# Batch 0 loaded by head halves, its first FFN tiles in another order, and batch 1's last 64 positions behind batch 2's keys by values

## The chip, the cores and the metric

The kernel runs on one core of one Trainium2 chip. The metric is the device time of an execution in microseconds. Lower is better. In this document PE is TensorE, DVE is VectorE, ACT is ScalarE, POOL is GpSimd and SP is SyncE.

## What is computed

The reference is a linear attention over 8 batches of 576 positions with 8 heads of 64, followed by a gated FFN on all 4608 positions:

```python
r = np.maximum(x, 0.0)                       # for q and for k
phi = np.concatenate([r * c, r * s], -1)     # c, s: cos and sin of pi/2 * position / S
kv = np.einsum('bhsf,bhsd->bhfd', k_p, v)    # keys by values, 128 x 64 a head
z = np.sum(k_p, axis=2)
num = np.einsum('bhsf,bhfd->bhsd', q_p, kv)
den = np.einsum('bhsf,bhf->bhs', q_p, z)[..., None] + 1e-06
x = (num / den)                              # to (4608, 512)
out = (gelu(x @ w_gate) * (x @ w_val)) @ w_out      # 512 -> 1536 -> 512
```

Inputs and output are 32-bit floats; the matmuls run on bf16.

## The kernel before

The program is written out by hand in its order: what the source issues first on an engine runs first there, and engines meet only through semaphores.

A batch has 576 positions in tiles t = 0 to 4 of 128, 128, 128, 128 and 64. For each batch, `sk` (L351) and `sq` (L348) scale k and q by the cosine (which = 0) and sine (which = 1) on VectorE ("v") or ScalarE ("s"), `cast_v` (L139) turns v into bf16, and `kv_half` (L151) multiplies keys by values for heads 0 to 3 or 4 to 7, 20 matmuls of 65 columns (the 65th column is the sum z). `numer` (L193) does the eight numerator matmuls of a tile (`numer_mm`, L168) and its normalisation (`norm`, L177: den, reciprocal, and a multiplication that writes the tile `xb`). Then x has to be transposed into `xT`, either on TensorE with an evacuation (`x_by_pe`, L336) or by a DMA from SP (`turn_x`, L201; for the last tile of a batch GpSimd copies the result into place, L209). q is transposed by TensorE (`q_by_pe`, L320, and `q_evac`, L328) or by DMA (`turn_q`, L143).

The FFN runs in blocks n of 576 (n = 0) or 512 positions and 12 tiles jt of 128 hidden columns. `gate` (L214) is four matmuls and a Gelu on ScalarE, `value` (L225) four matmuls and a product on VectorE into `hT`. `o_tile` (L266) is the 12 output matmuls for 128 positions. An output tile can begin 64 positions ahead of its block, so `carry(n)` (L242) has GpSimd copy the last 64 columns of block n's `hT` to the front of the other `hT` buffer.

Each `gate`, `value`, `numer` and transpose names its PSUM bank by hand. A matmul into a bank waits until the bank's last reader is done.

**The start.** The source loads batch 0 in this order on SP (one piece of k on ScalarE's queue): k of heads 0 to 3, k of heads 4 to 7, q of tiles 0 and 1, v of heads 0 to 3, v of heads 4 to 7, the rest of q. Each is two transfers (odd and even partitions). The weights come on GpSimd's queue (`load_w`, L304), held back by a small copy on ScalarE (L360) that waits for q. TensorE runs matmuls on zeros (`dummies`, L125) until real work is there, and a few between. Then batch 0's attention and block 0's FFN are interleaved by hand (L355 to L443), so that gates on the first positions begin while later tiles of x are still computed. In L401 to L407, `X(t, bank, engine)` is `x_by_pe` of tile t, and `Y(t, bank)` is `numer` of tile t.

**Block 0's end.** Batch 1's k and v are loaded behind a part of `w_out` (L449). After block 0's last value, batch 1's keys are scaled, its v cast, and its keys by values put between output tiles (L478 to L492). Batch 1's tiles 0 to 3 are computed there too; its tile 4 is left for block 1:

```python
    mid[1][3].append(L(attn_step, 1, 5))
```

`mid[n][jt]` is what runs between gate and value of tile jt in block n, `after[n][jt]` what follows the value. In block 1, batch 2's keys are scaled and its v cast in `after[1][0]` to `after[1][3]`, and its keys by values are in `after[1][4]` (banks 6 and 7). From block 2 on every block holds the same work for the next batch.

Of the kernel before, what the change touches and what calls it, by code (L numbers as in the profile page):

```python
# [10 lines left out]
BF16 = mybir.dt.bfloat16  # L11
# [5 lines left out]
def kernel(  # L17
# [19 lines left out]
    NJ = 4  # L37
# [50 lines left out]
    pos_i = sb.tile([128, NJ + 1], mybir.dt.int32, name="pos_i")  # L88
    par_i = sb.tile([128, 1], mybir.dt.int32, name="par_i")
    load(kf, k, 0, 0, 4, nc.scalar)  # L90
    load(kf, k, 0, 4, 8)
    nc.vector.memset(junk, 0.0)
    nc.gpsimd.iota(par_i, pattern=[[1, 1]], base=0, channel_multiplier=1)
    nc.gpsimd.iota(pos_i, pattern=[[2, NJ + 1]], base=0, channel_multiplier=9)
    half_pi = sb.tile([128, 1], FP32, name="half_pi")
    nc.gpsimd.memset(half_pi, math.pi / 2.0)
    nc.gpsimd.memset(qf[:, :, NJ], 0.0)
    nc.gpsimd.memset(vf[:, :, NJ], 0.0)
    load(qf, q, 0, j1=2)
    load(vf, v, 0, 0, 4)  # L100
    load(vf, v, 0, 4, 8)
    load(qf, q, 0, j0=2)

# [35 lines left out]
    def cast_v(b, h0, h1, eng="v"):  # L139
        cp = nc.vector.tensor_copy if eng == "v" else nc.scalar.copy  # L140
        cp(vx[b % 2][:, :, h0:h1, 0:D], vf[:, h0:h1].rearrange("p h j d -> p j h d"))  # L141
# [9 lines left out]
    def kv_half(b, g, bank, eng="s"):  # L151
        for h in range(4 * g, 4 * g + 4):
            for j in range(NJ + 1):
                nc.tensor.matmul(  # L154
                    ps[:, bank, (h % 4) * (D + 1):(h % 4 + 1) * (D + 1)],
                    lhsT=kp[:, j, h, :],
                    rhs=vx[b % 2][:, j, h, 0:D + 1],
                    start=(j == 0), stop=(j == NJ),
                )
        if eng is not None:  # L160
            kv_evac(b, g, bank, eng)

    def kv_evac(b, g, bank, eng):
        src = ps[:, bank, 0:4 * (D + 1)].rearrange("p (h e) -> p h e", e=D + 1)
        dst = kv[b % 2][:, 4 * g:4 * g + 4, 0:D + 1]
        (nc.scalar.copy if eng == "s" else nc.vector.tensor_copy)(dst, src)

    def numer_mm(b, t, bank, g, rows=128):  # L168
        for h in range(4 * g, 4 * g + 4):
            nc.tensor.matmul(  # L170
                ps[0:rows, bank + g, (h % 4) * (D + 1):(h % 4 + 1) * (D + 1)],
                lhsT=qT[b % 2][:, t, h, 0:rows],
                rhs=kv[b % 2][:, h, 0:D + 1],
                start=True, stop=True,
            )

    def norm(xb, bank, g0, g1, rows=128):  # L177

        n = g1 - g0
        nd = ps[0:rows, bank + g0:bank + g1, 0:4 * (D + 1)].rearrange("p g (h e) -> p g h e", e=D + 1)  # L180
        den = rot.tile([128, 2, 4], FP32, name="den")
        nc.vector.tensor_scalar(den[0:rows, 0:n], nd[:, :, :, D], EPS, None, op0=ALU.add)  # L182
        rec = rot.tile([128, 2, 4], FP32, name="rec")
        nc.vector.reciprocal(rec[0:rows, 0:n], den[0:rows, 0:n])
        nc.vector.tensor_tensor(  # L185
            xb[0:rows, g0:g1], nd[:, :, :, 0:D],
            rec[0:rows, 0:n, :, None].to_broadcast([rows, n, 4, D]), op=ALU.mult,
        )

    def new_xb():  # L190
        return rot.tile([128, 2, 4, D], BF16, name="xb", bufs=4)
# [33 lines left out]
    def value(n, jt, c0, w, vb):  # L225

        p0 = starts[n] + c0
        for ct in range(CT):
            nc.tensor.matmul(  # L229
                ps[:, vb, 0:w], lhsT=wv_sb[:, ct, jt * 128:(jt + 1) * 128],  # L230
                rhs=xT[:, ct, p0:p0 + w], start=(ct == 0), stop=(ct == CT - 1),
            )
# [95 lines left out]
    def q_evac(b, j, bank, eng, h0=0, h1=H):  # L328
        qb = ps[:, bank, :].bitcast(BF16).rearrange("p (h t) -> p h t", h=H)
        cp = nc.vector.tensor_copy if eng == "v" else nc.scalar.copy  # L330
        if j < NJ:
            cp(qT[b % 2][:, j, h0:h1], qb[:, h0:h1])  # L332
        else:
            cp(qT[b % 2][:, j, h0:h1, 0:64], qb[:, h0:h1, 0:128:2])

    def x_by_pe(b, t, xb, bank, eng, c0=0, c1=CT):  # L336
        p0 = b * S + t * 128
        cp = nc.vector.tensor_copy if eng == "v" else nc.scalar.copy
        xb2 = xb.rearrange("p g h d -> p (g h d)")
        rows = 128 if t < NJ else 64  # L340
        view = ps[:, bank, 0:256].bitcast(BF16).rearrange("p (c t) -> p c t", c=CT)
        for ct in range(c0, c1):
            nc.tensor.transpose(  # L343
                out=view[:, ct, 0:rows], in_=xb2[0:rows, ct * 128:(ct + 1) * 128], identity=ident[0:rows, 0:rows],
            )
        cp(xT[:, c0:c1, p0:p0 + rows], view[:, c0:c1, 0:rows])

    def sq(j, which, eng, *h):  # L348
        scale(Q, j, which, eng, *h)

    def sk(j, which, eng, *h):  # L351
        scale(K, j, which, eng, *h)


    dummies(26)  # L355
    for h0 in (0, 4):
        for j in range(NJ + 1):
            sk(j, 0, "v", h0, h0 + 4)
            sk(j, 1, "v" if j < 2 else "s", h0, h0 + 4)
    nc.scalar.copy(wg_sb[0:2, 0, 0:1], qf[0:2, 7, 1, D - 1:D])  # L360
    load_w(0, 2)
    load_w(2, 4)
    load_w(4, 8)
    for j in range(2):
        sq(j, 0, "v"), sq(j, 1, "s")
        q_by_pe(0, j, j, None)
    dummies(3)
    q_evac(0, 0, 0, "v")
    cast_v(0, 0, 2, "v")
    cast_v(0, 2, 4, "s")  # L370
    kv_half(0, 0, 4, None)
    q_evac(0, 1, 1, "v")
    dummies(2)
    cast_v(0, 4, 6, "v")
    cast_v(0, 6, 8, "s")
    kv_evac(0, 0, 4, "v")
    kv_half(0, 1, 5, "s")
    x0, x1 = new_xb(), new_xb()
    numer_mm(0, 0, 6, 0)
    norm(x0, 6, 0, 1)  # L380
    dummies(1, 4)
    numer_mm(0, 0, 6, 1)
    sq(2, 1, "s")
    norm(x0, 6, 1, 2)
    sq(2, 0, "v")
    numer_mm(0, 1, 0, 0)
    numer_mm(0, 1, 0, 1)
    norm(x1, 0, 0, 2)
    x_by_pe(0, 0, x0, 4, "s", 0, 2)
    dummies(2, 5)  # L390
    x_by_pe(0, 0, x0, 4, "s", 2, 4)
    q_by_pe(0, 2, 3, None)

    nc.gpsimd.tensor_copy(tiny[0:1, 1:2], x0[0:1, 1, 3, D - 1:D])
    load_w(8, 12)
# [5 lines left out]
    def X(t, bank, eng):  # L401
        return lambda: x_by_pe(0, t, xs[t], bank, eng)

    def Y(t, bank):
        def f():
            xs[t] = numer(0, t, bank, 128 if t < NJ else 64)
        return f  # L407

    gate(0, 0, 0, 128, 5)
    gate(0, 1, 0, 128, 4)  # L410
    X(1, 2, "s")()
    q_evac(0, 2, 3, "v")
    sq(3, 0, "v"), sq(3, 1, "s")
    value(0, 0, 0, 128, 6)
    value(0, 1, 0, 128, 7)
    Y(2, 0)()
    gate(0, 0, 128, 128, 5)
    gate(0, 1, 128, 128, 4)
    value(0, 0, 128, 128, 2)
    value(0, 1, 128, 128, 3)  # L420
    q_by_pe(0, 3, 6, "s")
    gate(0, 2, *A, 5)
    X(2, 0, "v")()
    sq(4, 1, "s"), sq(4, 0, "v")
    gate(0, 3, *A, 4)
    value(0, 2, *A, 7)
    Y(3, 0)()
    value(0, 3, *A, 2)
    q_by_pe(0, 4, 3, "s")
    gv_unit(0, 0, 256, 128, 5, 6)  # L430
    gv_unit(0, 1, 256, 128, 4, 7, (X(3, 0, "s"),))
    Y(4, 2)()
    gv_unit(0, 0, 384, 128, 5, 1)
    gv_unit(0, 1, 384, 128, 4, 0)
    gate(0, 4, *A, 5)
    X(4, 7, "v")()
    gate(0, 5, *A, 4)
    gv_unit(0, 2, *Bw, 2, 6)
    gv_unit(0, 3, *Bw, 3, 7)
    value(0, 4, *A, 1)  # L440
    value(0, 5, *A, 2)
    gv_unit(0, 0, 512, 64, 4, 6)
    gv_unit(0, 1, 512, 64, 5, 7)  # L443


    load_q(1, nc.gpsimd)
# [7 lines left out]
    def L(f, *a):  # L454
        return lambda: f(*a)


    def T(t, bank, eng):
# [7 lines left out]
        (9, 0): (L(sq, 4, 0, "v"), L(sq, 4, 1, "s"), ),  # L466
        (9, 1): (L(turn_q, 1, 2, 5), ),
        (10, 1): (L(load_q, 2), ),
        (11, 1): (L(carry, 0), ),
    }  # L470
    for jt in range(4, 12):
        for i, (c0, w) in enumerate((A, Bw)):
# [55 lines left out]
    after = {n: {jt: [] for jt in range(JT)} for n in range(NB)}  # L528

    mid = {n: {jt: [] for jt in range(JT)} for n in range(NB)}  # L530
    mid[1][3].append(L(attn_step, 1, 5))
    for n in range(1, 7):
        b = n + 1
        a = after[n]
# [75 lines left out]
```

## Time and profile before

| | us |
|---|---|
| median of 9 runs | 326.43 (326.0 to 326.72) |
| the profiled execution: device time | 326.58 |
| its span, first to last instruction | 324.8 |
| outside the span in that execution | 1.8 |
| first gate matmul of block 0 | 16.69 |
| first output matmul (end of block 0's FFN) | 44.51 |
| batch 1's keys by values | 48.74 |
| batch 2's keys by values | 67.60 |

The last four rows are start times in the profiled execution, in microseconds from the span's start, as are all times below that stand alone. In a line of the timeline the columns are: start, duration, engine, source line, operation, output<-inputs, shape, count, and in brackets the engine's idle time ahead of it with what ended it. A TensorE record begins when the matmul enters and ends when its last result is written, so records that follow each other overlap, and the distance from start to start says how long the queue is taken. A few matmul records are missing from a trace.

### The profile page before, as it was taken

The page shows a single profiled execution, that of the slowest core. Times are in us where ns is not written, and L with a number is a line of the kernel's source. Part 1 is how long each engine was busy: PE and PEld are TensorE (multiplying, and loading weights), DVE is VectorE, ACT ScalarE, POOL GpSimd, SP SyncE. Part 2 cuts the span into 40 slices and gives each one's busy share as a digit, 9 for nine tenths or more (in the row PEclk, how much of TensorE's full clock was granted, in tenths as well). Part 3 has the DMA queues.
Part 4 walks back from the last instruction along what each step waited for, and adds up shares of the span by engine and source line. Part 5 has one row for each costly group of instructions (what it writes and reads, how often), then busy time and mean ns, then how long its engine had stood idle before and what let it go on. Part 6 is the DMA issues. An engine that isn't in the chain of part 4 may idle for free.

```text
span 324.8 us, 5830 instructions
## 1 busy us (share of the span) xinstructions
PE 314.7 (97%) x2185; PEld 166.7 (51%) x2218; DVE 168.5 (52%) x380; ACT 151.4 (47%) x271; POOL 21.8 (7%) x43
## 2 busy tenths in 40 slices
PE   7899999999999999999999999999999999999994
PEld 3497866455445544554455445544554444444443
DVE  5885776777663575366636574637454222222210
ACT  6674774852583247325642565237522222323321
POOL 2651010000100010001000100010000100100000
PEclk9999999999999999999999999999999999999998
DMA  7999999999899929991999279936433111000124
GB/s 225 286 205 276 228 302 296 323 189 198 289 208 354 208 50 194 322 246 50 191 328 234 57 149 291 307 67 119 109 69 78 32 32 34 32 32 32 36 64 98
DMA packets 88300, 55.56 MB, mean 171 GB/s; under 512 B 53072, under 2 KB 83536, under 8 KB 88272
## 3 DMA queue, kind: packets, MB, share of 16 engines
q1 hardware_dynamic: 81744, 48.84, 60.8%
q0 software_dynamic: 6096, 5.90, 10.2%
q10 hardware_dynamic: 432, 0.46, 0.4%
q8 instruction: 17, 0.28, 0.3%
q14 instruction: 11, 0.09, 0.1%
HBM read 37.75 MB, written 9.44 MB: 145 GB/s over the span
## 4 chain that ended last, share of the span: by engine, by line
PE 91%; DVE 3%; DMA 2%; issue 1%; ACT 1%; POOL 0%; SPq 0%; DVEq 0%; POOLq 0%; ACTq 0%
PE ps L218 28%; PE ps L229 28%; PE ps L259 26%; PE ps L154 3%; PE ps L170 3%; DMA qf<-in_q_dram 2%; DVE kp L135 1%; PE ps L324 1%; DVE vx L141 1%; PE ps L277 1%; PE ps L343 1%; DVE xb L185 0%; SPq L80 0%; DVE qT L332 0%; ACT qp L137 0%
## 5 line engine op out<-in xcount | busy, mean ns | idle before, releaser
L234 DVE TENSOR_TENSOR hT<-gel,ps 128x512 bf16<-128x512 f32 (+5 forms) x126 | 76.1, 608 | 91.3 <-PE ps L229 90.8
L218 PE MATMUL ps<-xT,wg_sb 128*128 128x512 bf16 (+5 forms) x491 | 111.7, 348 | 0.8
L229 PE MATMUL ps<-xT,wv_sb 128*128 128x512 bf16 (+5 forms) x497 | 112.0, 348 | 0.4
L223 ACT ACTIVATE gel<-ps 128x512 f32<-128x512 f32 (+5 forms) x126 | 67.4, 536 | 73.9 <-PE ps L218 50.2
L259 PE MATMUL ps<-wo_sb,hT 128*128 128x512 bf16 x408 | 94.1, 379 | 0.6
L218 PEld LDWEIGHTS <-wg_sb 128*128 128x128 bf16 x504 | 47.1, 98 | 44.6
L229 PEld LDWEIGHTS <-wv_sb 128*128 128x128 bf16 x504 | 45.7, 98 | 39.0
L259 PEld LDWEIGHTS <-hT 128*128 128x128 bf16 x420 | 40.7, 98 | 47.7
L288 ACT COPY o_sb<-ps 128x512 f32<-128x512 f32 x35 | 20.5, 586 | 76.1 <-PE ps L259 74.9
L185 DVE TENSOR_TENSOR xb<-ps,rec 128x512 bf16<-128x512 f32 (+2 forms) x41 | 27.8, 678 | 2.2 <-DMA xr<-xb 0.7
L182 DVE TENSOR_SCALAR den<-ps 128x8 f32<-128x8 f32 (+2 forms) x41 | 6.7, 164 | 41.1 <-PE ps L170 41.1
L137 ACT ACTIVATE kp<-kf,sin_c 128x512 bf16<-128x512 f32 (+1 forms) x41 | 25.4, 681 | 0.7 <-DMA kf<-in_k_dram 0.7
L170 PEld LDWEIGHTS <-qT 128*128 128x128 bf16 (+1 forms) x320 | 15.1, 98 | 8.3 <-issue 0.4
L135 DVE TENSOR_SCALAR kp<-kf,cos_c 128x512 bf16<-128x512 f32 (+1 forms) x45 | 18.7, 463 | 1.3 <-DMA kf<-in_k_dram 1.3
L137 ACT ACTIVATE qp<-qf,sin_c 128x512 bf16<-128x512 f32 x28 | 19.3, 714 | 0.1
L135 DVE TENSOR_SCALAR qp<-qf,cos_c 128x512 bf16<-128x512 f32 x40 | 18.0, 491 | 0.3 <-DMA qf<-in_q_dram 0.3
L170 PE MATMUL ps<-kv,qT 128*128 128x65 bf16 (+1 forms) x320 | 16.6, 194 | 0.1
L209 POOL COPY xT<-xr 128x256 bf16<-128x256 bf16 x7 | 2.8, 402 | 198.4 <-DMA xr<-xb 198.4
L154 PEld LDWEIGHTS <-kp 128*128 128x128 bf16 x320 | 10.8, 97 | 3.3 <-issue 1.2
L154 PE MATMUL ps<-vx,kp 128*128 128x65 bf16 x320 | 11.1, 193 | 0.5 <-DVE xb L185 0.2
L127 PE MATMUL ps<-hT 128*128 128x512 bf16 x33 | 9.5, 434 | 1.8 <-DVE par_i L104 1.7
L141 ACT CAST vx<-vf 128x1280 bf16<-128x1280 f32 (+1 forms) x9 | 9.7, 1076 | 1.2 <-DMA vf<-in_v_dram 1.2
(54 smaller groups left out, 88.5 us busy)
## 6 DMA issues: line engine op xcount, KB each, us to landing
out_dram<-o_sb SPq DMA_DIRECT2D x38, 128.0 KB, 2.4
kf<-in_k_dram SPq DMA_DIRECT2D x7, 640.0 KB, 8.0
out_dram<-o_sb SPq DMA_DIRECT2D x16, 256.0 KB, 2.8
qf<-in_q_dram SPq DMA_DIRECT2D x6, 640.0 KB, 6.1
vf<-in_v_dram SPq DMA_DIRECT2D x6, 640.0 KB, 9.5
kf<-in_k_dram SPq DMA_DIRECT2D x7, 512.0 KB, 6.6
qf<-in_q_dram SPq DMA_DIRECT2D x6, 512.0 KB, 5.0
vf<-in_v_dram SPq DMA_DIRECT2D x6, 512.0 KB, 8.6
```

Source lines behind the costliest of these rows:

```text
L135: nc.vector.tensor_scalar(d, s, col, 0.0, op0=ALU.mult, op1=ALU.max)
L137: nc.scalar.activation(d, s, AF.Relu, scale=col)
L141: cp(vx[b % 2][:, :, h0:h1, 0:D], vf[:, h0:h1].rearrange("p h j d -> p j h d"))
L154: nc.tensor.matmul(ps[:, bank, (h % 4) * (D + 1):(h % 4 + 1) * (D + 1)], lhsT=kp[:, j, h, :], rhs=vx[b % 2][:, j, h, 0:D + 1], start=(j == ...
L170: nc.tensor.matmul(ps[0:rows, bank + g, (h % 4) * (D + 1):(h % 4 + 1) * (D + 1)], lhsT=qT[b % 2][:, t, h, 0:rows], rhs=kv[b % 2][:, h, 0:D ...
L185: nc.vector.tensor_tensor(xb[0:rows, g0:g1], nd[:, :, :, 0:D], rec[0:rows, 0:n, :, None].to_broadcast([rows, n, 4, D]), op=ALU.mult,)
L218: nc.tensor.matmul(ps[:, gb, 0:w], lhsT=wg_sb[:, ct, jt * 128:(jt + 1) * 128], rhs=xT[:, ct, p0:p0 + w], start=(ct == 0), stop=(ct == CT - 1),
L223: nc.scalar.activation(gel[:, 0:w], ps[:, gb, 0:w], AF.Gelu)
L229: nc.tensor.matmul(ps[:, vb, 0:w], lhsT=wv_sb[:, ct, jt * 128:(jt + 1) * 128], rhs=xT[:, ct, p0:p0 + w], start=(ct == 0), stop=(ct == CT - 1),
L234: nc.vector.tensor_mul(hT[n % 2][:, jt, 64 + c0:64 + c0 + w], gel[:, 0:w], ps[:, vb, 0:w])
L259: nc.tensor.matmul(ps[:, bank, :], lhsT=hT[n % 2][:, jt, c0:c0 + 128], rhs=wo_sb[:, jt, :], start=(jt == 0), stop=(jt == JT - 1),)
L288: nc.scalar.copy(o_sb, ps[:, bank, :])
```

## The change

It has two parts.

First, in block 1, tile 4 of batch 1 moves from between gate and value of jt = 3 to between gate and value of jt = 5, which is behind batch 2's keys by values, and takes bank 4 (and 5) instead of 5 (and 6). `carry(0)`, GpSimd's copy of block 0's last FFN columns, moves from block 0's last unit to the same place behind it.

Second, batch 0's loads are reordered: k of heads 0 to 3, q of tiles 0 and 1, v of heads 0 to 3, and only then k and v of heads 4 to 7. The work follows this order: heads 0 to 3 go up to the normalised first halves of tiles 0 and 1 before keys of heads 4 to 7 are scaled. The copy that holds back the weights waits for v of heads 0 to 3 instead of q, and stands behind a q evacuation on ScalarE. In block 0's FFN the order of gates, values, numerators and transposes, and their banks, change; `value` gets its product split off (`product`), and `x_by_pe` its evacuation (`x_evac`), so that the two halves can stand apart.

```diff
     load(kf, k, 0, 0, 4, nc.scalar)
-    load(kf, k, 0, 4, 8)
...
-    nc.gpsimd.memset(vf[:, :, NJ], 0.0)
     load(qf, q, 0, j1=2)
     load(vf, v, 0, 0, 4)
+    load(kf, k, 0, 4, 8)
     load(vf, v, 0, 4, 8)
     load(qf, q, 0, j0=2)
...
-    dummies(26)
-    for h0 in (0, 4):
-        for j in range(NJ + 1):
-            sk(j, 0, "v", h0, h0 + 4)
-            sk(j, 1, "v" if j < 2 else "s", h0, h0 + 4)
-    nc.scalar.copy(wg_sb[0:2, 0, 0:1], qf[0:2, 7, 1, D - 1:D])
-    load_w(0, 2)
-    load_w(2, 4)
-    load_w(4, 8)
+    dummies(19)
+    for j in range(NJ + 1):
+        sk(j, 0, "v", 0, 4)
+        sk(j, 1, "v" if j < 2 else "s", 0, 4)
     for j in range(2):
         sq(j, 0, "v"), sq(j, 1, "s")
         q_by_pe(0, j, j, None)
     dummies(3)
     q_evac(0, 0, 0, "v")
+    q_evac(0, 1, 1, "s", 0, 4)
+    nc.scalar.copy(wg_sb[0:2, 0, 0:1], vf[0:2, 3, 3, D - 1:D])
+    load_w(0, 2)
+    load_w(2, 4)
+    load_w(4, 8)
     cast_v(0, 0, 2, "v")
     cast_v(0, 2, 4, "s")
-    kv_half(0, 0, 4, None)
-    q_evac(0, 1, 1, "v")
+    q_evac(0, 1, 1, "v", 4, 8)
+    kv_half(0, 0, 4, "s")
     dummies(2)
+    x0, x1 = new_xb(), new_xb()
+    numer_mm(0, 0, 6, 0)
+    numer_mm(0, 1, 0, 0)
+    for j in range(NJ + 1):
+        sk(j, 0, "v", 4, 8)
+        sk(j, 1, "v" if j < 1 else "s", 4, 8)
+    norm(x0, 6, 0, 1)
     cast_v(0, 4, 6, "v")
     cast_v(0, 6, 8, "s")
-    kv_evac(0, 0, 4, "v")
+    dummies(8)
+    x_by_pe(0, 0, x0, 4, "s", 0, 2)
     kv_half(0, 1, 5, "s")
-    x0, x1 = new_xb(), new_xb()
-    numer_mm(0, 0, 6, 0)
-    norm(x0, 6, 0, 1)
-    dummies(1, 4)
+    norm(x1, 0, 0, 1)
+    sq(2, 0, "v"), sq(2, 1, "s")
+    dummies(1, 3)
+    x_by_pe(0, 1, x1, 2, None, 0, 2)
     numer_mm(0, 0, 6, 1)
-    sq(2, 1, "s")
     norm(x0, 6, 1, 2)
-    sq(2, 0, "v")
-    numer_mm(0, 1, 0, 0)
     numer_mm(0, 1, 0, 1)
-    norm(x1, 0, 0, 2)
-    x_by_pe(0, 0, x0, 4, "s", 0, 2)
-    dummies(2, 5)
+    norm(x1, 0, 1, 2)
+    dummies(1, 3)
     x_by_pe(0, 0, x0, 4, "s", 2, 4)
+    x_evac(0, 1, 2, "s", 0, 2)
     q_by_pe(0, 2, 3, None)
+    q_evac(0, 2, 3, "s", 0, 4)
...
     gate(0, 0, 0, 128, 5)
+    x_by_pe(0, 1, x1, 2, "v", 2, 4)
+    q_evac(0, 2, 3, "v", 4, 8)
     gate(0, 1, 0, 128, 4)
-    X(1, 2, "s")()
-    q_evac(0, 2, 3, "v")
-    sq(3, 0, "v"), sq(3, 1, "s")
-    value(0, 0, 0, 128, 6)
-    value(0, 1, 0, 128, 7)
-    Y(2, 0)()
-    gate(0, 0, 128, 128, 5)
-    gate(0, 1, 128, 128, 4)
-    value(0, 0, 128, 128, 2)
-    value(0, 1, 128, 128, 3)
-    q_by_pe(0, 3, 6, "s")
-    gate(0, 2, *A, 5)
-    X(2, 0, "v")()
+    sq(3, 0, "v")
+    gate(0, 0, 128, 128, 6)
+    gate(0, 1, 128, 128, 7)
+    sq(3, 1, "s")
+    value(0, 0, 0, 128, 0)
+    value(0, 1, 0, 128, 1)
+    Y(2, 2)()
+    value(0, 0, 128, 128, 5, False)
+    value(0, 1, 128, 128, 4, False)
+    gate(0, 2, *A, 7)
+    X(2, 2, "v")()
+    product(0, 0, 128, 128, 5)
+    product(0, 1, 128, 128, 4)
+    gate(0, 3, *A, 6)
+    q_by_pe(0, 3, 1, "s")
+    gate(0, 0, 256, 128, 3)
+    gate(0, 1, 256, 128, 5)
     sq(4, 1, "s"), sq(4, 0, "v")
-    gate(0, 3, *A, 4)
-    value(0, 2, *A, 7)
-    Y(3, 0)()
-    value(0, 3, *A, 2)
+    value(0, 2, *A, 0)
+    value(0, 3, *A, 4)
+    Y(3, 6)()
+    value(0, 0, 256, 128, 1)
+    value(0, 1, 256, 128, 2)
     q_by_pe(0, 4, 3, "s")
-    gv_unit(0, 0, 256, 128, 5, 6)
-    gv_unit(0, 1, 256, 128, 4, 7, (X(3, 0, "s"),))
-    Y(4, 2)()
-    gv_unit(0, 0, 384, 128, 5, 1)
-    gv_unit(0, 1, 384, 128, 4, 0)
-    gate(0, 4, *A, 5)
-    X(4, 7, "v")()
+    gate(0, 4, *A, 0)
+    X(3, 6, "s")()
     gate(0, 5, *A, 4)
-    gv_unit(0, 2, *Bw, 2, 6)
+    gate(0, 0, 384, 128, 5)
+    Y(4, 1)()
+    value(0, 0, 384, 128, 7)
+    gv_unit(0, 1, 384, 128, 3, 6)
+    value(0, 4, *A, 4)
+    X(4, 1, "v")()
+    value(0, 5, *A, 0)
+    gv_unit(0, 2, *Bw, 2, 5)
     gv_unit(0, 3, *Bw, 3, 7)
-    value(0, 4, *A, 1)
-    value(0, 5, *A, 2)
-    gv_unit(0, 0, 512, 64, 4, 6)
-    gv_unit(0, 1, 512, 64, 5, 7)
+    gv_unit(0, 0, 512, 64, 1, 6)
+    gv_unit(0, 1, 512, 64, 2, 4)
...
-        (11, 1): (L(carry, 0), ),
...
-    mid[1][3].append(L(attn_step, 1, 5))
+    mid[1][5].append(L(attn_step, 1, 5, 4))
+
+    mid[1][5].append(L(carry, 0))
```

A and Bw are positions 0 to 255 and 256 to 575 of the block.

More of the change, by code (lines that the diff above doesn't have):

```diff
@@ L96 @@
     nc.gpsimd.memset(half_pi, math.pi / 2.0)
+    nc.gpsimd.memset(vf[:, :, NJ], 0.0)
     nc.gpsimd.memset(qf[:, :, NJ], 0.0)
-    nc.gpsimd.memset(vf[:, :, NJ], 0.0)
     load(qf, q, 0, j1=2)
     load(vf, v, 0, 0, 4)
+    load(kf, k, 0, 4, 8)
     load(vf, v, 0, 4, 8)
@@ L223, in gate, with value @@
         nc.scalar.activation(gel[:, 0:w], ps[:, gb, 0:w], AF.Gelu)
-    def value(n, jt, c0, w, vb):
+    def value(n, jt, c0, w, vb, now=True):
         p0 = starts[n] + c0
@@ L232, in value, with product @@
             )
+        if now:
+            product(n, jt, c0, w, vb)
+    def product(n, jt, c0, w, vb):
         gel = gels.pop((n, jt, c0))
@@ L336, in x_by_pe @@
     def x_by_pe(b, t, xb, bank, eng, c0=0, c1=CT):
-        p0 = b * S + t * 128
-        cp = nc.vector.tensor_copy if eng == "v" else nc.scalar.copy
         xb2 = xb.rearrange("p g h d -> p (g h d)")
@@ L345, in x_by_pe, with x_evac @@
             )
+        if eng is not None:
+            x_evac(b, t, bank, eng, c0, c1)
+    def x_evac(b, t, bank, eng, c0=0, c1=CT):
+        p0 = b * S + t * 128
+        cp = nc.vector.tensor_copy if eng == "v" else nc.scalar.copy
+        rows = 128 if t < NJ else 64
+        view = ps[:, bank, 0:256].bitcast(BF16).rearrange("p (c t) -> p c t", c=CT)
         cp(xT[:, c0:c1, p0:p0 + rows], view[:, c0:c1, 0:rows])
```

## The prediction

> **What bounds the kernel now.** I read the page's busy shares and slices first, then TensorE's timeline, then the other engines at each place where TensorE has a gap.
>
> ```profile
> PE 314.7 (97%) x2185; PEld 166.7 (51%) x2218; DVE 168.5 (52%) x380; ACT 151.4 (47%) x271; POOL 21.8 (7%) x43
> PE   7899999999999999999999999999999999999994
> ```
>
> TensorE is the bound, and only gaps in its queue can be won or lost. The page's "busy" hides most gaps, because a matmul's record outlives its place in the queue; I read gaps from start to start. In the steady blocks a 512-column matmul starts every 0.216 us, a 128-column one every 0.055, a 65-column one every 0.031. From batch 3's keys by values (97.86) to batch 4's (131.42) it takes 33.56 us; 24 units of 0.864, four output tiles of 2.59, 1.21 for keys by values and five numerators of 0.25 make 33.57. So from block 2 on there is no gap, and a shift made earlier is carried to the end. What is left are the first gate at 16.69, gaps in block 0, and two waits:
>
> ```profile
> 16.69 0.61 PE L218 MATMUL ps<-xT,wg_sb 128*128 128x128 bf16 x8
> ...
> 20.11 0.39 PE L343 MATMUL ps<-ident,xb 128*128 128x128 bf16 x4
> ...
> 23.02 0.39 PE L343 MATMUL ps<-ident,xb 128*128 128x128 bf16 x4
> 23.24 0.39 PE L229 MATMUL ps<-xT,wv_sb 128*128 128x128 bf16 x4
> 23.56 0.44 PE L170 MATMUL ps<-kv,qT 128*64 128x65 bf16 x8
> 24.08 0.38 PE L218 MATMUL ps<-xT,wg_sb 128*128 128x128 bf16 x4
> ...
> 48.74 1.37 PE L154 MATMUL ps<-vx,kp 128*128 128x65 bf16 x40 [0.18 <-DVE vx L141]
> ```
>
> The eight 65-column matmuls at 23.56 fill 0.25, to 23.81; the next gate starts at 24.08: a gap of 0.27. Found so, block 0's gaps are 0.14 (17.27), 0.14 (18.34), 0.10 (23.56), 0.27 (24.08), 0.10 (25.50): 0.75. At 48.74 the queue was free from 44.51 + 18 x 0.216 = 48.40: 0.34. The third place is batch 2's keys by values:
>
> ```profile
> 66.35 1.03 PE L229 MATMUL ps<-xT,wv_sb 128*128 128x512 bf16 x4
> 67.60 1.37 PE L154 MATMUL ps<-vx,kp 128*128 128x65 bf16 x40 [0.23 <-DVE xb L185]
> ```
>
> Queue free at 66.35 + 0.86 = 67.21: a gap of 0.39, ended by the normalisation of batch 1's last 64 positions, which still reads bank 6.
>
> **What the Trainium skill says.** "TensorE: Matmul & The Clock Gate", Back-to-back issue gap: N/2.4 + 2.5 ns, so 216 and 56 ns; the trace agrees (0.216, 0.055). Same page, What's actually happening: the array falls to half clock after about 3.4 us of idling. No gap that I find below is longer than 0.8 us, so I count no clock loss. "DMA: Bandwidth & Descriptors", Issuing engines are not separate DMA queues: transfers of all queues share 16 engines. The trace agrees: the DMA slices stand at 9 from 3 to 48 us, so reordering loads moves landings and not their sum. "GPSIMD Engine Reference", Specifications: GpSimd shares SBUF interfaces with VectorE in two-port modes. The trace shows it:
>
> ```profile
> L135 DVE TENSOR_SCALAR kp<-kf,cos_c x5: 475/476/1048, 45.2 to 47.3; 128x512 bf16<-128x512 f32 x5
> ```
>
> One of five equal instructions took 1048 ns instead of 476, while GpSimd's carry (L245) ran from 45.33 for 1.02 us.
>
> **Part 1, work behind batch 2's keys by values.** The carry leaves VectorE's chain before batch 1's keys by values: 1048 - 475 = 0.57 us. That chain ended 48.70 and would end 48.1; the queue's 48.40 and ScalarE's last scaled key (48.50, used by the fifth matmul) then decide. Gain 0.25 of the 0.34. The carry's new place on GpSimd is behind the L209 copy (77.16, 0.40 us), so about 77.6 to 78.6; its reader is the output tile at 85.61: cover 7 us. VectorE then works from PSUM (L185, L234); 0 taken, at most 0.4.
>
> The numerator of 8 x 0.031 moves, its 0.25 us stays on TensorE. At 67.21 - 0.25 = 66.96 VectorE's cast (65.57 + 0.95 = 66.52) is done, and the second head half follows 0.6 later, at 67.56, when ScalarE's cast (65.83 + 1.27 = 67.10) is done. So the 0.39 goes: gain 0.35, 0 to 0.39. Its normalisation, 1.1 us, comes to about 70.1 to 71.2, where VectorE idled 2.06 us before 70.80; what is late next is the numerator at 71.64, which takes the same banks, with 0.4 to spare. Its DMA transpose is still behind load_q(3) on SP's queue; it was issued at 71.29 with its data ready since 67.55, and now gets them at about 71.2, so its landing (77.1) and the xb buffer that waits for it hardly move. Block 2's first gate (82.16) needs the last transpose of batch 2, landed 80.65: 1.5 us of cover. Part 1: -0.6 (0 to -0.75).
>
> **Part 2a, the start.** Landings before: q 9.15, v of heads 0 to 3 at 10.80, k of 4 to 7 at 7.48, v of 4 to 7 at 12.49 (issue 6.24 + 6.3). With k's second half (1.8 us of transfer) behind, I estimate q 7.3, v 9.0, k 10.7, v 12.5. The seven dummies dropped (7 x 0.216) were idle time: real work waits for q. Turning q (10.09) comes to 8.05, heads 0 to 3's keys by values end near 11. But now two engines have work waiting for the late k:
>
> - ScalarE: evacuate kv to 11.5, four scaled halves of 0.41 to 13.1, its cast 0.72 to 13.8.
> - VectorE: six scaled halves of 0.265 from 10.75 to 12.35, normalisation 0.83 to 13.1, its cast 0.56 to 13.7.
>
> So the second keys by values starts at 13.7, before at 13.28. Then kv 14.5 to 14.9, numerator 14.95, normalisation to 16.10, transposes, evacuation 16.45 to 16.82, gate 16.86: before 16.69. The gain of the earlier q and v is spent here: **+0.2** (-0.4 to +0.5). The weights' first issue moves behind ScalarE's q half and v's landing, 9.72 to about 10.1; the shared engines make it up, and wg (9.72 + 5.9 = 15.6) has 1 us of cover. The loads' new order on SP costs nothing by itself (an issue takes 0.65 us, 3 to 6 us ahead of its landing), nor does the swap of GpSimd's memsets of v and q (0.52 each, done at 2.0 before; v is issued from 2.9 on).
>
> **Part 2b, block 0's order.** Prices: numerator to finished xb 1.68 us (17.95 to 19.63 in the trace: 0.41 for the last result, den, reciprocal, 0.69); transposes to evacuated xT and the next gate 1.06 (23.02 to 24.08). A gap is such a price less the work put between:
>
> - Gate on positions 128 to 255: VectorE normalises until 16.87, the second pair of transposes comes at 17.15, evacuation 17.47 to 17.76: gap 0.3 + 0.1.
> - X(2): between its numerator and it stand 0.25 + two values 0.44 + a gate 0.43 = 1.12: gap 0.5. Before, 0.25 + four of 0.22 + 0.45 + 0.43 = 2.0 covered it.
> - Turning q's last 64: ScalarE has a 1.0 evacuation and two gelus ahead of sq(4) and ends it 0.3 after TensorE is there.
> - Gate at 384: between X(3) and it 0.22 + 0.43 = 0.65 of 1.06, and a gelu is ahead: gap 0.5.
> - X(4): 0.25 + 3 x 0.22 + 0.43 = 1.34 of 1.68: gap 0.3.
> - Gate(2) on 256 to 575: behind X(4) 0.65 of work, and VectorE does a product of 0.42 ahead of the evacuation: gap 0.3.
>
> Sum 2.3, less 0.75 = **+1.5**; the waits overlap in part and gates begin with two of four tiles, so I take +1.3 (+0.7 to +1.9). Weights stay covered: wg of tiles 4 to 7 land near 22.2, used at 24.
>
> **Sum.** +0.2 +1.3 -0.6 = +0.9. The span goes 324.8 to 325.7, the profiled execution 326.58 to 327.5; that one lies 0.15 above the median of 326.43, so the median goes to 327.3. Gains ahead of 48 us would be capped too: batch 1's k lands at 44.50 and ScalarE needs 3.7 us from there; a loss has no cap.
>
> **Rivals.** (A) 65%: as above, 326.8 to 328.3. (B) 23%, nearly nothing: block 0's new gaps are worth only 0.6, because half of the listed latencies overlap; 326.43 + 0.6 - 0.6 = 326.4. For it: the first-tile work is spread finer; against: VectorE was already 86% busy from 17 to 24 us, so late results are not caught up. (C) 12%, faster: the first gate comes earlier. Place: the second keys by values. If q and v land a further 0.7 earlier, or k does, and both engines have drained when v's second half lands (12.5), it starts at 13.1, the first gate at 16.2; with block 0's gaps at +0.4 the sum is -0.5 + 0.4 - 0.6 = -0.7: 325.7. It decides once 2a and 2b together are under 0; against it, ScalarE's backlog to 13.8 depends little on the landings. (D) inside A: the moved normalisation collides with batch 2's at 71 us; +0.4.
>
> **Numbers.** 0.2% is 0.65 us, about what a measurement of this kernel can tell from no change. A is over it in most of its range (0.63 of the total), B lies within it, C under it. Range 326.0 to 328.3: it takes in B and leaves out C's core and A's far end.
>
> **What would show it.** Right: first gate at 16.7 to 17.2; gaps before X(2) and before the gate at 384; the last value of block 0 more than 0.7 later than 43.97; five scaled keys at 475 ns; no VectorE wait before batch 2's keys by values. Wrong: first gate before 16.4, or block 0's gaps under 1.2 us in sum.

## The result, and the profile after

The changed kernel takes 328.56 us (median of 9 runs, 328.14 to 329.02), the kernel before 326.43 (29 runs). The ratio is 1.0065, with a 95% interval of 1.0057 to 1.0074: slower by 2.1 us, where the forecast was 0.9. The profiled execution took 328.27 us, its span 326.4 (before 326.58 and 324.8).

The page's busy shares and slices of the changed kernel:

```profile
PE 315.8 (97%) x2184; PEld 167.2 (51%) x2218; DVE 167.7 (51%) x382; ACT 152.3 (47%) x275; POOL 21.8 (7%) x43
PE   7899999999999999999999999999999999999994
```

Nothing on this page tells the two kernels apart: the shares and every digit of TensorE's row are as before. As in the prediction, the change has to be read from start to start in TensorE's timeline. Here are the places of the changed block 0 where the queue stood open:

```profile
17.18 0.45 PE L218 MATMUL ps<-xT,wg_sb 128*128 128x128 bf16 x4
17.63 0.27 PE L345 MATMUL ps<-ident,xb 128*128 128x128 bf16 x2
17.74 1.11 PE L218 MATMUL ps<-xT,wg_sb 128*128 128x128 bf16 x12
18.69 0.61 PE L229 MATMUL ps<-xT,wv_sb 128*128 128x128 bf16 x8
...
20.79 0.40 PE L345 MATMUL ps<-ident,xb 128*128 128x128 bf16 x4 [0.35 <-DVE xb L185]
...
24.13 0.62 PE L328 MATMUL ps<-ident,qp 128*128 128x128 bf16 x8
...
26.18 0.38 PE L218 MATMUL ps<-xT,wg_sb 128*128 128x128 bf16 x4 [0.34 <-ACT xT L356]
...
28.21 0.29 PE L345 MATMUL ps<-ident,xb 64*128 64x64 bf16 x4
28.43 0.61 PE L229 MATMUL ps<-xT,wv_sb 128*128 128x256 bf16 x4
29.13 0.70 PE L218 MATMUL ps<-xT,wg_sb 128*128 128x320 bf16 x4
```

The reader is to take each start and subtract the time at which the matmuls before it have passed the queue. The twelve gate matmuls at 17.74 have passed at 17.74 + 12 x 0.055 = 18.40, and the value comes at 18.69: 0.28 is lost inside that row, ahead of the gates on positions 128 to 255. In the same way 0.23 is lost between 17.18 and 17.63. The further gaps are 0.52 at 20.79 (tile 2's x is not normalised yet), 0.20 at 24.13 (q of the last tile), 0.50 at 26.18 (the gate on 384 to 511), 0.22 and 0.09 at tile 4's transposes, 0.25 at 29.13, and 0.19 in two small ones. They sum to 2.48; before, the same count gave 0.79. So the gaps make block 0 longer by 1.69. By its ends it is 1.60 longer: from first gate to first output tile it took 27.82 before (16.69 to 44.51) and 29.42 after (17.18 to 46.60). Two of tile 1's four transposes (0.11) now run ahead of the first gate, which makes up most of the difference.

Batch 1's keys by values start at 50.48, batch 2's at 68.77, both with no wait named in the row; the waits for VectorE ahead of them are gone. The last output tiles (`o_last`) begin 1.42 later than before, at 318.75 where it was 317.33. The span is 1.6 longer, so 0.2 more came after that.

### The profile page after: what moved, and what is told of

It is laid out like the page before. It is cut to its first block, busy times and chain, and to the rows that moved or that the text cites. A ratio compares the mean times of both kernels' runs of the same rounds, so it can differ in the third digit from the quotient of the medians.

```text
span 326.4 us, 5832 instructions
## 1 busy us (share of the span) xinstructions
PE 315.8 (97%) x2184; PEld 167.2 (51%) x2218; DVE 167.7 (51%) x382; ACT 152.3 (47%) x275; POOL 21.8 (7%) x43
## 4 chain that ended last, share of the span: by engine, by line
PE 94%; DVE 3%; issue 1%; ACT 1%; DVEq 0%; ACTq 0%
PE ps L218 28%; PE ps L229 28%; PE ps L263 28%; PE ps L170 3%; PE ps L154 3%; PE ps L127 2%; PE ps L328 1%; PE ps L281 1%; DVE kp L135 1%; PE ps L345 1%; DVE vx L141 0%; DVE hT L238 0%; DVE xb L185 0%; ACT gel L223 0%; DVE rec L184 0%
## 5 line engine op out<-in xcount | busy, mean ns | idle before, releaser
L170 PEld LDWEIGHTS <-qT 128*128 128x128 bf16 (+1 forms) x320 | 15.2, 98 | 8.6 <-issue 0.6
L135 DVE TENSOR_SCALAR kp<-kf,cos_c 128x512 bf16<-128x512 f32 (+1 forms) x45 | 18.4, 459 | 0.9 <-DMA kf<-in_k_dram 0.9
L135 DVE TENSOR_SCALAR qp<-qf,cos_c 128x512 bf16<-128x512 f32 x40 | 17.7, 485 | 0.2 <-DMA qf<-in_q_dram 0.2
L127 PE MATMUL ps<-hT 128*128 128x512 bf16 x32 | 10.4, 479 | 1.8 <-DVE par_i L104 1.7
```

The lines of the kernel that those rows point to most:

```text
L135: nc.vector.tensor_scalar(d, s, col, 0.0, op0=ALU.mult, op1=ALU.max)
L170: nc.tensor.matmul(ps[0:rows, bank + g, (h % 4) * (D + 1):(h % 4 + 1) * (D + 1)], lhsT=qT[b % 2][:, t, h, 0:rows], rhs=kv[b % 2][:, h, 0:D ...
```

## The experiments

All comparisons are with the kernel before, run beside each of them on the same chip (326.4 to 326.5 each time).

**Part 1 alone, on the kernel before.**

```diff
-        (11, 1): (L(carry, 0), ),
...
-    mid[1][3].append(L(attn_step, 1, 5))
+    mid[1][5].append(L(attn_step, 1, 5, 4))
+    mid[1][5].append(L(carry, 0))
```

> The kernel before with only the first part of the change: tile 4 of batch 1 and carry(0) behind batch 2's keys by values. Theory (the parts add up; part 1 closes TensorE's two gaps ahead of keys by values, 0.34 and 0.39 us in the trace of before): 0.5 to 0.75 us faster than before, about 325.8; in its profile batch 1's keys by values start near 48.45 and block 2's first gate near 81.5. Rival 1 (only the gap at batch 2's closes, since ScalarE's last scaled key is ready no earlier): 0.35 us faster, 326.1. Rival 2 (the moved normalisation collides with batch 2's and costs what it gains): no change.

Measured: 325.85 us (21 runs), ratio 0.9984 (0.9977 to 0.9990): 0.61 less than before. TensorE's timeline of this kernel, the keys by values of batches 1 and 2:

```profile
48.01 0.29 PE L154 MATMUL ps<-vx,kp 128*128 128x65 bf16 x4
48.45 1.26 PE L154 MATMUL ps<-vx,kp 128*128 128x65 bf16 x36 [0.16 <-ACT kp L137]
...
66.57 1.37 PE L154 MATMUL ps<-vx,kp 128*128 128x65 bf16 x40
```

The wait for VectorE's cast has gone from the first row. The four matmuls at 48.01 end their place at 48.13; the fifth, which needs ScalarE's last scaled key, starts at 48.45, so 0.32 comes back as a wait for ScalarE. At 66.57 the queue goes straight on from a value at 65.71 (plus 4 x 0.216): the 0.39 of batch 2 is gone.

**Part 2 alone** (the changed kernel with those lines put back).

```diff
+        (11, 1): (L(carry, 0), ),
...
-    mid[1][5].append(L(attn_step, 1, 5, 4))
-    mid[1][5].append(L(carry, 0))
+    mid[1][3].append(L(attn_step, 1, 5))
```

> The changed kernel without its first part: batch 0's loads, start and block 0's order as changed, tile 4 of batch 1 and carry(0) where they were. Theory (the parts add up): 328.56 plus 0.5 to 0.75, so 329.1 to 329.3, or 2.6 to 2.9 us slower than before. Rival (part 1 is worth nothing once block 0 ends late, because batch 1's k and v have landed long before): 328.6.

Measured: 329.12 us (5 runs), ratio 1.0083 (1.0071 to 1.0096): +2.66. Against the whole change (+2.13) this gives part 1 a worth of about 0.5 inside it too, though the ends of the two kernels differ (below). Both waits (0.18 for the cast, 0.23 for batch 1's last `xb`) are back in its timeline. So the loss is all in part 2, and the next two runs split it.

**The start alone**: loads and first work as changed, block 0's order from the second gate on as before, no part 1.

```diff
     gate(0, 0, 0, 128, 5)
+    gate(0, 1, 0, 128, 4)
     x_by_pe(0, 1, x1, 2, "v", 2, 4)
     q_evac(0, 2, 3, "v", 4, 8)
-    gate(0, 1, 0, 128, 4)
...
+    sq(3, 0, "v"), sq(3, 1, "s")
+    value(0, 0, 0, 128, 6)
...
```

> The kernel before with the changed loads and start up to the first gate, but block 0's gates, values and transposes in the order of before (only tile 1's second transposes and evacuations stay split as in the change); tile 4 of batch 1 and carry(0) where they were. Theory (the order of block 0 is the larger loss, 1.6 us of the trace, the start the smaller): 0.3 to 0.7 us slower than before, 326.7 to 327.1, first gate near 17.1. Rival (the start costs more than its first gate tells, because TensorE's clock comes up late in some runs or tiles of x come late): 1.0 us slower or more, 327.4 and up.

Measured: 327.16 us (10 runs), ratio 1.0023 (1.0014 to 1.0032): +0.70, the upper end of the forecast. Its first gate is at 17.55, later than the 17.1 expected, and its end is 0.23 shorter than in the kernel before (below), so the start itself costs about 0.9. The rival's 1.0 and more did not come.

**The order alone**: the start of before, block 0 in the changed order from positions 128 on.

```diff
-    sq(3, 0, "v"), sq(3, 1, "s")
-    value(0, 0, 0, 128, 6)
...
+    sq(3, 0, "v")
+    gate(0, 0, 128, 128, 6)
+    gate(0, 1, 128, 128, 7)
+    sq(3, 1, "s")
...
```

> The kernel before with its loads and start, but block 0 in the changed order from the gates on positions 128 to 255 on (tile 1 of x is turned and evacuated as in before). Theory (block 0's order costs 1.3 to 1.7 us, by waits for normalised and evacuated tiles of x): 1.3 to 1.9 us slower than before, 327.8 to 328.3, with gaps before X(2), before the gate at 384 and around X(4). Rival (the order is only bad behind the changed start, since that delivers tiles of x later): 0.5 us slower or less, 326.9.

Measured: 328.52 us (5 runs), ratio 1.0065 (1.0052 to 1.0077): +2.06, more than forecast. TensorE's timeline of this kernel:

```profile
16.63 0.61 PE L218 MATMUL ps<-xT,wg_sb 128*128 128x128 bf16 x8
17.21 0.40 PE L347 MATMUL ps<-ident,xb 128*128 128x128 bf16 x4
18.29 0.61 PE L218 MATMUL ps<-xT,wg_sb 128*128 128x128 bf16 x8 [0.67 <-ACT xT L350]
...
20.89 0.40 PE L347 MATMUL ps<-ident,xb 128*128 128x128 bf16 x4 [0.41 <-DVE xb L185]
```

The gates on positions 128 to 255 were pulled ahead of the values, so they stand right behind the transposes that they need. These have passed the queue at 17.21 + 0.22 = 17.43, and the gate waits for the evacuated `xT` until 18.29: 0.84 to 0.86, with nothing to run in between. With the changed start half of tile 1 is transposed earlier, and the gaps around this gate are 0.51 in sum. The others (0.58, 0.20, 0.50, 0.56) are nearly those of the changed kernel. From first gate to first output tile this kernel takes 30.07 (16.63 to 46.70), 2.25 more than before.

**Weights late, in the kernel of the start alone.** This asks why the start costs more than forecast.

```diff
     nc.scalar.copy(wg_sb[0:2, 0, 0:1], vf[0:2, 3, 3, D - 1:D])
-    load_w(0, 2)
-    load_w(2, 4)
-    load_w(4, 8)
...
     nc.gpsimd.tensor_copy(tiny[0:1, 1:2], x0[0:1, 1, 3, D - 1:D])
+    load_w(0, 2)
+    load_w(2, 4)
+    load_w(4, 8)
     load_w(8, 12)
```

> The changed start with block 0's order of before (as e3_start), and all weight loads moved on GpSimd's queue behind the first normalised tile, so that GpSimd prepares no transfer before about 16.6 us. Its time is of no interest (block 0 waits for weights); the second keys by values (heads 4 to 7) is. Theory (VectorE's scaled keys of heads 4 to 7 and its cast of v, which took up to 601 and 832 ns instead of 347 and 549, are slowed by GpSimd preparing the weight transfers at the same time): all six take about 347 ns and the cast 549, and the keys by values of heads 4 to 7 start by 13.8, against 14.07, 14.17 and 14.54 in the three runs with this start. Rival (the slow instructions have another cause, and ScalarE's casts set the time): VectorE's durations still spread to 600, or the keys by values stay at 14.1 or later.

Its time (333.0 us, one execution) says nothing here, since the first gate waits for the weights; it is read only up to the second keys by values. GpSimd's timeline of the changed kernel shows it writing weight transfers from 10.60 to 15.2 without a pause, two of the six being:

```profile
11.49 0.75 POOL L310 DMA_DIRECT2D wv_sb<-in_moe_w_val_dram  x1
12.23 0.76 POOL L309 DMA_DIRECT2D wg_sb<-in_moe_w_gate_dram  x1
```

VectorE's timeline of the changed kernel, in the same stretch:

```profile
10.84 0.35 DVE L135 TENSOR_SCALAR kp<-kf,sin_c 128x256 bf16<-128x256 f32 x1
11.10 1.52 DVE L135 TENSOR_SCALAR kp<-kf,cos_c 128x256 bf16<-128x256 f32 x4
...
13.28 0.83 DVE L141 CAST vx<-vf 128x640 bf16<-128x640 f32 x1
```

And with the weights late:

```profile
10.89 0.35 DVE L135 TENSOR_SCALAR kp<-kf,sin_c 128x256 bf16<-128x256 f32 x1
11.15 1.14 DVE L135 TENSOR_SCALAR kp<-kf,cos_c 128x256 bf16<-128x256 f32 x4
...
12.94 0.55 DVE L141 CAST vx<-vf 128x640 bf16<-128x640 f32 x1
```

The same four scaled keys take 1.52 or 1.14 us, the same cast 0.83 or 0.55. Not every operation is hit: the key at 10.84 takes 0.35, although GpSimd's first weight transfer was being prepared from 10.60 on. Heads 4 to 7 land no earlier with the weights late (k at 10.52, v at 12.20; in the changed kernel 10.46 and 12.16), so it is not that the weights take a share of the DMA engines. Nor is it the weights' data: in the changed kernel their first packet moves at 12.65, when the six keys are done (12.62). What slows VectorE is GpSimd's preparation of the weight transfers. How much, the other profiles with the changed start tell, from the start of the first key of heads 4 to 7 to the end of VectorE's cast:

| kernel | first key starts | cast ends | takes | second keys by values | first gate |
|---|---|---|---|---|---|
| weights late | 10.62 | 13.49 | 2.87 | 13.74 | waits for weights |
| part 2 alone | 10.54 | 14.02 | 3.48 | 14.07 | 17.08 |
| changed kernel | 10.58 | 14.11 | 3.53 | 14.17 | 17.18 |
| changed, two clears (below) | 10.78 | 14.26 | 3.48 | 14.31 | 17.33 |
| start alone | 10.73 | 14.48 | 3.75 | 14.54 | 17.55 |
| changed, second profile (below) | 10.68 | 14.62 | 3.94 | 14.66 | 17.68 |
| tile 2 later (below) | 10.82 | 14.62 | 3.80 | 14.67 | 17.68 |

With the weights in their place VectorE takes 0.6 to 1.1 us longer, the keys by values start about 0.05 after its cast, and the first gate follows 3.01 to 3.02 later. These keys by values are 0.3 to 0.9 later than with GpSimd quiet, 0.7 in the mean. With GpSimd quiet they gain less than VectorE does, because something else holds them until 13.74: TensorE's own queue, with eight matmuls on zeros and two transposes.

```profile
11.90 1.89 PE L127 MATMUL ps<-hT 128*128 128x512 bf16 x8
13.62 0.27 PE L345 MATMUL ps<-ident,xb 128*128 128x128 bf16 x2
13.74 0.77 PE L154 MATMUL ps<-vx,kp 128*128 128x65 bf16 x20
```

So it is partly luck that 13.74 is the 13.7 of the prediction, which had VectorE's cast as what they wait for; VectorE was done at 13.49.

**Part 1 with one scaled key of ScalarE ahead of an output tile's evacuation**, against the 0.32 that came back in part 1 alone.

```diff
-    o_tile(0, 0, 4)
     sk(NJ, 1, "s")
+    o_tile(0, 0, 4)
```

> e1_part1 with batch 1's last scaled key (sk(4, 1) on ScalarE) ahead of the evacuation of the first output tile on ScalarE instead of behind it. Theory (in e1_part1 TensorE stands 0.3 us inside batch 1's keys by values for that key): 0.3 us faster than e1_part1, 325.55, 0.9 below before; the fifth matmul no longer waits. Rival (VectorE's cast of v is next and ends at about the same time): 0 to 0.1 us faster than e1_part1.

Measured: 325.77 us (10 runs), ratio 0.9976 (0.9967 to 0.9985). In its timeline all forty matmuls run through from 48.38:

```profile
48.38 1.37 PE L154 MATMUL ps<-vx,kp 128*128 128x65 bf16 x40
```

Yet the median is only 0.1 below part 1 alone, and the intervals overlap. That is the size of the rival's forecast, though its cause, a wait for VectorE's cast, is not in the timeline. The wait went; that it was worth its 0.3 is not shown. In the profile of part 1 alone the first gate came at 16.30, and ScalarE then waited 0.53 for batch 1's k to land before its first scaled key (44.75). In this one, with a first gate at 16.67, it didn't wait (44.58). So part of the 0.32 was a start that came early and met the landing, and batch 2's keys by values stand at 66.57 and 66.60 in the two.

**The changed kernel once more**, to see whether its profiled execution, 0.3 under its median, misleads.

> The changed kernel once more, unaltered, for a second profile and more timed runs. Theory (the 0.4 us by which the medians differ more than the two profiled executions do are scatter of the start and of the last stores' landing): median 328.3 to 328.7; first gate between 17.0 and 17.6, landing of the last store 2.2 to 3.0 us after its issue. Rival (timed executions are slower than profiled ones for this kernel alone): the profiled execution is again 0.3 us under the median.

Measured: 328.85 us (5 runs), ratio 1.0064 (1.0050 to 1.0077); its profiled execution stands at its median, so the rival fell. Median and first gate came a little above the forecast: the span is 327.0 and the first gate at 17.68 instead of 17.18. So one kernel's start differs by 0.5 from execution to execution. VectorE's timeline shows where:

```profile
10.68 0.67 DVE L135 TENSOR_SCALAR kp<-kf,cos_c 128x256 bf16<-128x256 f32 x1 [0.24 <-DMA kf<-in_k_dram]
...
11.53 1.59 DVE L135 TENSOR_SCALAR kp<-kf,cos_c 128x256 bf16<-128x256 f32 x4
...
13.78 0.84 DVE L141 CAST vx<-vf 128x640 bf16<-128x640 f32 x1
```

The first key starts 0.10 later than in the first profile and takes 0.67 instead of 0.34: GpSimd's first transfer is being prepared from 10.37 on, ahead of that key, where it was 10.60. So what differs from one execution to the next is which operations of VectorE fall on this preparation. The start therefore has to be averaged over several profiles. The twelve profiles of this study with the weights in their place, those of the next runs among them, give:

| first gate | profiles | mean |
|---|---|---|
| start of before | 16.69, 16.30, 16.63, 16.67, 16.49, 16.39 | 16.53 |
| changed start | 17.18, 17.08, 17.55, 17.68, 17.68, 17.33 | 17.42 |

The two sets don't overlap: the start costs 0.9.

**Tile 2's transposes moved behind one more gate.** This tries one line of the list of gaps.

```diff
-    X(2, 2, "v")()
     product(0, 0, 128, 128, 5)
     product(0, 1, 128, 128, 4)
     gate(0, 3, *A, 6)
+    X(2, 2, "v")()
```

> The changed kernel with tile 2's transposes moved behind the gate of hidden tile 3 (256 columns, 0.43 us of TensorE) in block 0. Theory (a gap is the 1.6 us from a numerator to its normalised tile, less the work between): the gap of 0.52 before X(2) closes to about 0.1, no later gap grows, 0.4 us faster than the changed kernel, 328.1. Rival (the waits are one chain on VectorE: closing one moves it to the next, the gate at 256 or the last q): less than 0.1 us faster, 328.5.

Measured: 327.77 us (7 runs), ratio 1.0034 (1.0023 to 1.0046), about 0.8 to 1.1 less than the changed kernel. Its TensorE timeline:

```profile
20.34 1.04 PE L218 MATMUL ps<-xT,wg_sb 128*128 128x256 bf16 x8
21.29 0.40 PE L345 MATMUL ps<-ident,xb 128*128 128x128 bf16 x4
21.52 0.61 PE L328 MATMUL ps<-ident,qp 128*128 128x128 bf16 x8
22.20 0.61 PE L218 MATMUL ps<-xT,wg_sb 128*128 128x128 bf16 x8
...
26.38 0.38 PE L218 MATMUL ps<-xT,wg_sb 128*128 128x128 bf16 x4 [0.24 <-ACT xT L356]
```

The gap of 0.52 ahead of tile 2's transposes shrinks to 0.08 (20.34 + 8 x 0.109 = 21.21). But the gate that reads tile 2 now stands nearer to its transposes and waits 0.23 (21.52 + 0.44 = 21.96, start 22.20), and 0.20 opens ahead of tile 3's. The net up to batch 1's keys by values is 0.31 (50.67 against 50.98 in the second profile of the changed kernel, which has the same first gate, 17.68). The gain in the median is about three times that, and the spans of these two profiles differ by 0.85. Something after that point differed as well.

**The end of the kernel.** From the issue of the last store (on ScalarE's queue) to its landing:

| kernels | us | in the trace |
|---|---|---|
| before; part 1; start alone; order alone; key first; tile 2 later | 1.99 to 2.00 | no fetch of instructions among the last stores |
| changed kernel, its repeat, part 2 alone | 2.49, 2.63, 2.83 | a fetch among them |

The expectations below count, from the same issue, to the landing of the last store of all, one on SP's queue: 2.25 in the first row, 2.67 to 3.02 in the second.

The profile's rows for the transfers of the last 2 to 3 us, first of the kernel before, then of the changed one (queue, kind, packets, MB, share of the engines; then the last store with its median time to landing):

```profile
q10 hardware_dynamic: 160, 0.13, 20.2%
q1 hardware_dynamic: 158, 0.13, 19.3%
...
out_dram<-o_sb ACTq DMA_DIRECT2D x1, 64.0 KB, 2.0
```

```profile
q14 instruction: 1, 0.01, 1.1%
...
out_dram<-o_sb ACTq DMA_DIRECT2D x1, 64.0 KB, 2.5
```

q14 carries a block of 8192 bytes of instructions. In the changed kernel it starts at 323.3, between the last stores' packets. The trace counts VectorE's stream, with its semaphore instructions: 577 in the kernel before, part 1 alone and key first, 576 in the order alone, 578 in the three kernels with the long store, 580 in the start alone and with tile 2 later. The fetch comes after the last store with 576 and 577, and at about 312 to 313 with 580. VectorE's timeline of the changed kernel has the reason why one or two instructions can move it by 10 us:

```profile
311.25 0.62 DVE L238 TENSOR_TENSOR hT<-gel,ps 128x448 bf16<-128x448 f32 x1 [0.89 <-PE ps L229]
320.60 0.29 DVE L286 COPY o_sb<-ps 128x128 f32<-128x128 f32 x1 [8.73 <-ACT o_sb L285]
321.87 0.29 DVE L286 COPY o_sb<-ps 128x128 f32<-128x128 f32 x1 [0.97 <-ACT o_sb L285]
```

VectorE idles for 8.73 us there. If a fetch is due after so many instructions, it falls ahead of this idle time or behind it, by a count of one or two. The Trainium skill, "Runtime: NRT & Kernel Launch", Instruction fetch mechanics, says that each engine's sequencer fetches the next block through its own DMA queue while it executes, and that this is mostly hidden; it gives 16 KiB a block, where the trace shows 8192 bytes in q14 (and 16384 in the other instruction queue, q8). Three kernels test this. Each adds clears of one element on VectorE near its start, where it is idle, and nothing waits for them:

```diff
     nc.vector.memset(junk, 0.0)
+    pad = sb.tile([1, 4], FP32, name="pad")
+    nc.vector.memset(pad[:, 0:1], 0.0)
+    nc.vector.memset(pad[:, 1:2], 0.0)
```

Two clears in the changed kernel (578 to 580):

> The changed kernel with two one-element clears on VectorE added near its start, where VectorE is idle; nothing waits for them. VectorE's stream goes from 578 instructions to 580. Theory (where a block of instructions is fetched decides the tail): the 8192-byte fetch that began among the last stores (323 to 324 us) comes at about 312 us, as in the two kernels with 580; the time from the last store's issue to its landing falls from 2.7-2.8 to about 2.25 us, and the kernel is 0.4 to 0.6 us faster than the changed one: about 328.1, ratio to before about 1.005. Rival (the longer last store has another cause, such as the state of the stores of these three kernels): fetch or not, last store still 2.6 us or more, 328.6, ratio 1.0065.

Measured: 327.92 us (5 runs), ratio 1.0042 (1.0028 to 1.0057) where the changed kernel has 1.0065. The fetch comes at 313.1; the last store:

```profile
out_dram<-o_sb ACTq DMA_DIRECT2D x1, 64.0 KB, 2.0
```

One clear in the kernel before (577 to 578):

> The kernel before with one one-element clear on VectorE added near its start; nothing waits for it. VectorE's stream goes from 577 instructions to 578. Theory: the 8192-byte fetch, which came after the end of the kernel before, begins among the last stores; the last store takes 2.6 to 3.0 us from issue to landing where it took 2.25, and the kernel is 0.4 to 0.7 us slower than before: 326.8 to 327.1, ratio 1.0012 to 1.002. Rival (nothing but some 0.06 us of VectorE's idle time is spent): last store 2.25 us, ratio 1.000.

Measured: 326.82 us (13 runs) against 326.5, ratio 1.0008 (0.9999 to 1.0016). The fetch comes at 321.7, among the last stores:

```profile
q14 instruction: 1, 0.01, 0.9%
...
out_dram<-o_sb ACTq DMA_DIRECT2D x1, 64.0 KB, 2.5
```

Three clears in the kernel with the key first (577 to 580):

> Part 1 with the early scaled key of ScalarE, and three one-element clears on VectorE near its start: 580 instructions. Control for the other two: three clears more than the kernel of 325.8, so if clears as such cost anything it would show most here. Theory (the place of the fetch decides, 580 has it at about 312 us): last store 2.25 us, within 0.2 us of 325.8, ratio to before 0.9975 to 0.9985. Rival (each clear costs by itself, about as much as a 578-instruction stream): 326.2 or more, ratio 0.9995 or more.

Measured: 325.70 us (6 runs), ratio 0.9969 (0.9958 to 0.9981), against 0.9976 without the clears. The fetch comes at 310.5, the last store takes 1.99.

The place of the fetch and the landing of the last store follow the count in all three, in both directions: that is shown. How much of it reaches the time is smaller. From the last store's issue to the end of the span it is 4.0 us with 577 (the fetch comes just ahead of the end, at 324.7 of 324.8 in the kernel before), 4.2 to 4.5 with 578, 3.7 to 3.8 with 580, and 3.8 with the 576 of the order alone, whose fetch falls behind the end. So 578 should cost 0.2 to 0.5 against 577, and 580 gain about 0.2. The measured differences have these signs: +0.3 for one clear, -0.2 for the key first, and -0.6 to -0.9 for the changed kernel with two clears, where the ends differ by 0.5 to 0.6. But the interval of the kernel before with one clear holds no change, so the medians alone don't prove it. The spans agree to 0.01 for tile 2 later, which has 580: against the second profile of the changed kernel, 0.31 in block 0 and 0.55 at the end make 0.86, and 0.85 is the difference. The forecast of 0.4 to 0.7 for that kernel was too high: I had taken the whole longer landing as time.

The last kernel, part 1 with the key first and three clears, is the fastest of all, 0.3% faster than the kernel before.

## Why the prediction was wrong

Its direction, its list of gaps and part 1 were right; its sum was less than half of what came, and 328.56 lies above its range. By its terms:

| term | predicted | measured | by |
|---|---|---|---|
| start | +0.2 | +0.9 | twelve profiles' first gates; start alone +0.70, with an end shorter by 0.23 in it |
| block 0's order | +1.3 | +1.6 | first gate to first output tile; order alone, with its 0.84, +2.06 |
| part 1 | -0.6 | -0.6 | part 1 alone |
| end of the kernel | 0 | +0.2 | last store's issue to the span's end, 3.98 to 4.21 |
| sum | +0.9 | +2.1 | change measured: +2.13 |

- **The start, the step that failed most.** The landings were right: q 7.28, v 8.88, k 10.46, v 12.16 against 7.3, 9.0, 10.7 and 12.5. So was the list of work behind the late k. What failed is the price in "six scaled halves of 0.265 ... its cast 0.56". The keys' price came from a stretch in which GpSimd was quiet, the cast's from the shorter of two (0.55 and 0.64 before), and I put both where GpSimd prepares the weight transfers. The keys of heads 4 to 7 were scaled from 7.58 to 9.4 before, ahead of the weights' first issue at 9.72; the change moved them to 10.6 to 12.5, under it. From the first of these keys to the end of the cast the prediction had 2.95 us (10.75 to 13.7). With the weights late it is 2.87; with them in place 3.48 to 3.94, 3.66 in the mean of six. These 0.7 are the miss: the second keys by values start at 14.40 in the mean instead of 13.7. I had even quoted the row that shows the effect, a scaled key of 1048 ns beside GpSimd's copy, and used it for part 1 only. From there on the prediction held: 3.0 us from the second keys by values to the first gate, where it had 3.2. A smaller part of the miss is the reference: the six starts of the kernel before average 16.53, and the profile that I worked from shows 16.69.
- **Block 0's order.** The listed gaps held one by one: 0.4, 0.5, 0.3, 0.5, 0.3, 0.3 were forecast, and 0.51, 0.52, 0.20, 0.50, 0.31, 0.25 came (2.29 of 2.3). The step that failed is the sentence after them, "the waits overlap in part ... so I take +1.3": nothing overlapped, since each gap stands in TensorE's own queue at another place. The sum as it stood was +1.5. Rival B, which gave half of it back, fell with the same reading.
- **Part 1.** Right, by its own steps: five scaled keys at 481 ns and no slow one (VectorE's line of L135 from 44 to 50 us, in the changed kernel), no wait for VectorE ahead of batch 2's keys by values, and a new wait for ScalarE's last key ahead of batch 1's in part 1 alone. Nothing of rival D's collision is there: from batch 2's keys by values to batch 3's it takes 30.36 us in part 1 alone and 30.10 before, and the moved numerator is 0.25.

```profile
L135 DVE TENSOR_SCALAR kp<-kf,cos_c x5: 481/481/482, 47.3 to 48.9; 128x512 bf16<-128x512 f32 x5
```

- **The end.** The prediction took what lies behind the last matmul as fixed. It isn't; 0.2 us of the loss came from where a fetch of instructions fell, which follows the count of VectorE's instructions and not what they do.
- **Rival C**, a first gate before 16.4, fell: no changed start came before 17.08.
- **No clock loss** held: the granted clock is full in the changed kernel from 7.2 to 324.6. The half clock that the prediction counted out shows only with the weights late, where TensorE waits 4.01 us for them and the granted clock is 0.5 from 18.9 to 25.7.

The range failed because its terms were wrong to the same side: +0.7 at the start, +0.3 in block 0 and +0.2 at the end.

## What to carry to other kernels

A duration belongs to its neighbours: when a step is moved under GpSimd's preparation of DMAs, take VectorE's prices from a place where that was going on, or add the difference. Gaps that stand at different places of the bounding engine's own queue add up, and a sum of them is not to be shaded for overlap; but closing one can open the next, as with tile 2 later, where 0.31 was left of 0.44. When a change of less than 0.5 us can't be traced to any gap, compare the last store's time from issue to landing before looking for a cause in the change.

## What the runs showed of the hardware

- VectorE's scaling and casting from SBUF to SBUF is slowed while GpSimd writes weight transfers: four scaled keys 1.52 us instead of 1.14, a cast 0.83 instead of 0.55, and 0.6 to 1.1 us from the first key to the end of the cast. The Trainium skill, "SBUF — State Buffer", SBUF: two separate sides, says that GpSimd can't write the descriptors of its DMAs while VectorE runs an operation in a two-port mode, and that the ports which the two share go to whichever starts first, while the other blocks. The traces show VectorE as one that pays, and 0.14 to 0.32 us as the price of most operations that are hit, well under the 0.75 of one transfer's preparation. Whether these operations run in a two-port mode no run here shows.
- A fetch of 8192 bytes of instructions among the last stores makes the last one land after 2.5 to 2.8 us instead of 2.0, and one instruction more or less on VectorE decides whether it falls there.
- The first gate of one and the same kernel came at 17.18 and at 17.68 in two profiles; a single pair of profiles would have put the cost of the start anywhere from 0.4 to 1.4.
